# Sparse attention into a feed-forward network on one core: new costs and tables for the planner that orders the engines

## The chip, the core and the metric

The kernel runs on one core of one Trainium2 chip. The metric is the device time of one launch in microseconds (us), as a median of runs; for the kernel before it is 835.81 us (835.47 to 837.34, 3 runs). The engines are TensorE (PE; its weight loads are shown apart as PEld), VectorE (DVE), ScalarE (ACT), GpSimd (POOL), and SyncE (SP), which here only issues DMAs.

## The reference

```python
scores = scale * np.matmul(q, k.transpose(0, 1, 3, 2))    # B=8, H=8, S=576, D=64
mask_local = (rel >= 0) & (rel < 32)                      # heads 0 to 3
mask_strided = (rel >= 0) & (same residue modulo 32)      # heads 4 to 7
attn = softmax(where(mask, scores, -1e9))
x = matmul(attn, v), rearranged to 4608 tokens x 512
h = x @ w_in                                              # 512 x 2048
g = h * (1.0 / (1.0 + np.exp(-h)))
out = g @ w_out                                           # 2048 x 512
```

## The kernel before

**Arithmetic.** Every fp32 operand of the feed-forward products is split into a rounded upper part and a remainder, and a product is three matmuls (upper times upper, upper times lower, lower times upper). The upper part is a cast on ACT, the lower a subtraction on DVE: `ghi` (L757) and `glo` (L761) for the gated hidden values, `xop` pieces (L1440, L1456 on ACT, then DVE) for the first product's operands.

**Blocks.** The 4608 tokens are nine blocks of 512. For each of 16 chunks of the hidden width, blocks 0 and 1 do a first product (`hidden`, L717), a tanh (L727), a gating on DVE (L749), the two parts of the result, and a second product of 12 matmuls into four output banks (L776), which lags by one chunk. Blocks 2 to 4 take chunks two at a time by a scheme of seven half-size products, `p1` to `p7` (`multiply`, L1540, 256 columns a matmul), whose results ACT copies and DVE adds (copies L1791, L1795, L1798; tanh L1555). The words of `ORDER` and `BURST_ORDER` give the order of these seven and of the four quarters `0` to `3` of the lagging second product. A pair of chunks is called a step here; it has an index j from 0 to 7. Blocks 5 to 8 go in two pairs with 512 columns a matmul and seven products in both layers (L1540, L2093, L2222); `SUPER_ORDER` and `SUPER_BURST` give their words, and a copy on ACT (L1928) stands between some products that use the same bank.

**Weight sums.** The seven-product scheme needs sums of weight quarters. They are made during block 1, for eight f: POOL adds (L1295 to L1309), ACT casts the upper part into a slot of `xop` (L1319), DVE makes the lower (L1323), and SP stores the slot to DRAM (`keep_sum`, L1328, buffer `sums`, 512 KB each, two for each f). `xop` has six slots; four of them hold block 1's operands, so two are left, and a slot is free only when its store has landed. Later SP loads the sums into a ring (L1246). Sums for the second layer (`sum_outs`, L1379 to L1409) are made later at the steps in `OUT_SUMS`.

**Attention.** The attention of later blocks is inserted in bursts of two groups at the steps in `BURSTS` (`burst_jobs`, L1571). A burst's PE part has scores (L459, L468) and products with the values (L632) for the groups whose softmax is done. After it come DVE maxima, ACT exponentials (L526, each with a read of its sum), DVE scaling and transposes, and ACT copies of the transposed blocks (L599, to `pt`), which the *next* burst's L632 reads. ACT copies of the results are L644 and L672. ACT also moves finished output blocks from their banks to `stage` (L789), which SP stores.

**Order.** The first 130 us follow a written plan. All that follows is a list of `Job`s, each with an engine, a cost in us and the jobs it waits for; `in_order` (L1106) gives each a due time, counted back from the PE's jobs, and then plays the engines: PE's jobs in the written order, and on another engine, out of the first `LOOK` jobs, those that could start within `GRAIN` of the earliest, the one due first. Each engine executes its instructions strictly in the order so found, so a wait of the first holds up all behind it. An SP job costs `SP_ISSUE` of its queue and ends a fixed 5.0 later:

```python
firsts.append(min((f for f in found if f[0] <= start + GRAIN), key=lambda f: f[1].due))
...
free[j.engine] = t + SP_ISSUE if j.engine == "SP" else j.end
```

Of the kernel before, what the change touches and what calls it, by code (L numbers as in the profile page):

```python
# [65 lines left out]
BURSTS = {1: (1, 6, 11), 2: (1, 3, 5, 7), 3: (1, 3, 5, 7), 4: (1, 3, 5, 7), 5: (1, 3, 5)}  # L66
XORDER = ("b21", "b11", "t3", "t2", "t1", "t4", "b22")
ORDER = "p1 p7 p2 p6 0 p5 p4 1 p3 2 3"
BURST_ORDER = "0 p1 1 p7 p6 p2 p4 p5 2 3 p3"
SUPER_LAG = "p1 x x p2 p6 p7 x x p5 p4"  # L70
SUPER_FIRST = "p1 p7 p6 p2 p4 p5"
SUPER_ORDER = "p1 p7 p2 p6 p3- p4 p5"
SUPER_BURST = "p1 p3- p2 p7 B p6 p4 p5"
# [3 lines left out]
OUT_SUMS = {(2, 2): 0, (2, 4): 1, (2, 6): 2, (3, 0): 3, (3, 2): 4, (3, 6): 5, (4, 2): 6, (4, 4): 7}  # L77
# [8 lines left out]
FIRST_ORDER = "0 p7 1 p1 p2 p6 2 p5 p4 p3 3"  # L86
LOOK = 30
GRAIN = 0.04
SP_ISSUE = 0.1
# [111 lines left out]
def sparse_attention_ffn(ctx: ExitStack, tc: tile.TileContext, kqt, vt, w_in, w_out, out):  # L201
# [833 lines left out]
    class Job:  # L1035
        def __init__(self, engine, cost, act, after):
            self.engine, self.cost, self.act = engine, cost, act
            self.after, self.takes, self.late = [j for j in after if j], [], 0.0
            self.at = self.end = self.due = None
# [66 lines left out]
    def in_order():  # L1106
# [24 lines left out]
        for _ in range(PASSES):  # L1131
# [24 lines left out]
        while len(order) < len(jobs):  # L1156
# [12 lines left out]
            free[j.engine] = t + SP_ISSUE if j.engine == "SP" else j.end  # L1169
# [53 lines left out]
    def stream_on(n, p):  # L1223

        m = n + (RING if n < wide_first else WIDER)
        if m < n_sums:
            sum_loads[m] = job("SP", 5.0, lambda: load_sum(m), p, *kept_of(m))
# [56 lines left out]
    def sum_weights(f):  # L1284
# [55 lines left out]
        for i in range(2):  # L1340
# [3 lines left out]
            out.append(job("SP", 5.0, lambda i=i: keep_sum(i), l, ends=u.takes))  # L1344
# [3 lines left out]
    def sum_outs(f):  # L1348
# [51 lines left out]
        return [job("SP", 5.0, keep_sums, *l, ends=ends), kept_early.get(f) or keep_outs(f, *l)]  # L1400

    def keep_outs(f, *after):
# [8 lines left out]
        return job("SP", 5.0, act, *after)  # L1411
# [153 lines left out]
    def loads_behind(kind, i, after):  # L1565
        bufs, one = (KBUFS, load_qk) if kind == "k" else (VBUFS, load_v)
        i += bufs
        if i < len(groups) and (kind, i) not in loaded:
            loaded[kind, i] = job("SP", 5.0, lambda: one(groups[i]), after)

    def burst_jobs(c, between=lambda: None, pool="ps"):  # L1571
# [27 lines left out]
        for i, pe in zip((c, c + 1), pes):  # L1599
            value, later = groups[i], groups[i + 2] if i + 2 < len(groups) else None  # L1600
            cost = 0.33 if value.g.local else 0.62
# [8 lines left out]
            each = 0.336 if later.wide else 2 * dve(n * later.seen) / n  # L1610
            peaks = []
# [5 lines left out]
            each = 0.56 if later.wide else 0.525  # L1617
# [4 lines left out]
        for i, later, first, exps in soft:  # L1622
            n = later.g.n
            local = later.g.local
            total = job("DVE", 0.38, later.total, *exps)
# [4 lines left out]
            each = 0.36 if local else 0.43  # L1630
            turns = [job("DVE", 3 * each, lambda a=later: a.turn_in_place(), last, takes=["pt"])]
            for odd in (1, 0):
                turns.append(job("ACT", 2 * (act_of(2 * n * STRIDE)),
# [707 lines left out]
```

## Time and profile before

| | us |
|---|---|
| median of 3 runs (lowest to highest) | 835.81 (835.47 to 837.34) |
| the profiled execution, its own time | 835.76 |
| its span | 833.8 |
| PE busy | 814.8 |
| DVE busy | 632.9 |
| ACT busy | 559.7 |
| POOL busy | 70.3 |
| DMA | 182.78 MB, mean 219 GB/s |
| mean granted clock of PE | 0.992 |

The span runs from the first to the last instruction of one profiled execution; the execution's own time has some 2 us around it. A busy time says how much an engine did, not what the end waited for; that is read from the waits of PE, from the chain of waits that ended last, and from timelines of the engines where a wait stands. In a timeline, the bracket behind a row gives the idle time of that engine just before it, and what ended it.

### The profile page before, as it was taken

The numbers are of one execution on the slowest core, as the hardware profiler recorded it, in microseconds if no ns is written. First come the engines' busy times: TensorE is split into PE (matmuls) and PEld (weight loads), VectorE is DVE, ScalarE is ACT, GpSimd is POOL, SyncE is SP. The second block draws the span as 40 slices with busy tenths as digits, with TensorE's granted clock in tenths as the row PEclk, the third lists the DMA queues.
The fourth block names the chain that finished last, engine by engine and source line by source line (L and its number), as shares of the span: only waits on it lengthen the run. The fifth ranks groups of instructions, "written<-read, shape, count | busy, mean of one in ns | idle before, by whom it ended". The sixth has DMA issues, their size and how long they took to land.

```text
span 833.8 us, 19462 instructions
## 1 busy us (share of the span) xinstructions
PE 814.8 (98%) x7041; PEld 688.8 (83%) x7041; DVE 632.9 (76%) x1571; ACT 559.7 (67%) x1560; POOL 70.3 (8%) x122
## 2 busy tenths in 40 slices
PE   8899999999799999999999999999999999999998
PEld 5788878888598988888888988888888888888887
DVE  6899896675577777777778758777789984779853
ACT  7899875564677678777777768888555534555551
POOL 5300004675000000000000000000000000000000
PEclk9999999999899999999999999999999999999999
DMA  8876444378578776688876775876666788666676
GB/s 254 306 261 218 146 156 147 137 262 291 174 253 260 243 240 204 220 261 277 266 238 222 248 236 191 255 211 181 194 193 199 212 225 239 197 192 191 192 219 156
DMA packets 139007, 182.78 MB, mean 219 GB/s; under 512 B 29408, under 2 KB 82272, under 8 KB 138912
## 3 DMA queue, kind: packets, MB, share of 16 engines
q1 hardware_dynamic: 137392, 180.82, 69.8%
q8 instruction: 56, 0.92, 0.4%
q10 hardware_dynamic: 1520, 0.72, 0.3%
q14 instruction: 39, 0.32, 0.1%
HBM read 142.70 MB, written 38.80 MB: 218 GB/s over the span
## 4 chain that ended last, share of the span: by engine, by line
PE 91%; DMA 4%; ACT 2%; DVE 1%; SPq 1%; issue 1%; POOL 0%; ACTq 0%; POOLq 0%; DVEq 0%
PE ps L1540 33%; PE po L776 25%; PE po L2093 13%; PE ps L717 9%; PE ps L2093 4%; DMA sums<-xop 2%; PE ps L632 2%; PE ps L468 2%; PE po L2222 1%; DMA k<-kqt 1%; PE ps L459 1%; PE ps L885 1%; ACT pt L599 1%; PE po L632 0%; SPq L385 0%
## 5 line engine op out<-in xcount | busy, mean ns | idle before, releaser
L1540 PE MATMUL ps<-xop,w 128*128 128x256 f32 (+1 forms) x1152 | 182.6, 310 | 0.0
L1540 PEld LDWEIGHTS ps<-xop,w 128*128 128x128 f32 x1152 | 165.7, 191 | 15.5
L526 ACT ACTIVATE sm<-sm,sums 128x54 f32<-128x54 f32 (+2 forms) x320 | 109.4, 344 | 5.5 <-DVE sums L508 5.4
L717 PE MATMUL ps<-xop,w 128*128 128x512 f32 x384 | 95.2, 396 | 0.0
L776 PE MATMUL po<-w,ghi 128*128 128x512 f32 x280 | 88.5, 398 | 6.0 <-ACT ghi L757 6.0
L1540 PE MATMUL ps<-w,w 128*128 128x512 f32 x384 | 91.2, 390 | 0.0
L717 PEld LDWEIGHTS ps<-xop,w 128*128 128x128 f32 x384 | 71.8, 190 | 15.5
L1540 PEld LDWEIGHTS ps<-w,w 128*128 128x128 f32 x384 | 71.8, 188 | 14.9
L761 DVE TENSOR_TENSOR glo<-th,ghi 128x512 fp32r<-128x512 f32 x80 | 57.6, 722 | 21.2 <-ACT ghi L757 20.7
L776 PEld LDWEIGHTS po<-w,ghi 128*128 128x128 f32 x280 | 52.1, 192 | 16.1 <-ACT ghi L757 6.4
L526 ACT ACTIVATION_READ_ACCUMULATOR sm<-sm,sums 128x1 f32 x320 | 60.5, 189 | 0.0
L757 ACT CAST ghi<-th 128x512 fp32r<-128x512 f32 x78 | 48.1, 619 | 17.4 <-PE po L776 11.1
L776 PE MATMUL po<-w,glo 128*128 128x512 f32 x140 | 55.3, 395 | 0.2 <-DVE glo L761 0.2
L776 PE MATMUL po<-stage,ghi 128*128 128x512 f32 x160 | 50.5, 397 | 0.0
L2093 PE MATMUL po<-stage,w 128*128 128x512 f32 x210 | 49.2, 389 | 0.0
L2093 PEld LDWEIGHTS po<-stage,w 128*128 128x128 f32 x210 | 39.4, 188 | 8.2
L599 ACT COPY pt<-sm 32x192 f32<-32x192 f32 (+1 forms) x102 | 36.9, 362 | 2.6 <-DVE sm L591 0.4
L2093 PE MATMUL po<-v,w 128*128 128x512 f32 x162 | 38.3, 389 | 0.0
L486 POOL MEMSET sm<- 128x80 f32 (+1 forms) x18 | 2.9, 161 | 420.6 <-ACT pt L599 244.8
L776 PE MATMUL po<-v,ghi 128*128 128x512 f32 x120 | 37.9, 397 | 0.0
L749 DVE SCALAR_TENSOR_TENSOR th<-th,ps 128x512 f32<-128x512 f32 x32 | 21.6, 681 | 20.1 <-ACT th L727 20.1
L2093 PEld LDWEIGHTS po<-v,w 128*128 128x128 f32 x162 | 30.4, 188 | 6.3
(278 smaller groups left out, 1626.8 us busy)
## 6 DMA issues: line engine op xcount, KB each, us to landing
w<-sums SPq DMA_DIRECT2D x232, 256.0 KB, 2.9
w<-osums SPq DMA_DIRECT2D x104, 256.0 KB, 2.9
sums<-xop SPq DMA_DIRECT2D x16, 512.0 KB, 3.5
osums<-stage SPq DMA_DIRECT2D x16, 512.0 KB, 3.9
v<-vt SPq DMA_DIRECT2D x21, 384.0 KB, 4.0
stage<-w_out SPq DMA_DIRECT2D x14, 512.0 KB, 4.2
k<-kqt SPq DMA_DIRECT2D x14, 477.0 KB, 5.6
stage<-w_in SPq DMA_DIRECT2D x12, 512.0 KB, 4.4
```

The source lines that it names most:

```text
L459: nc.tensor.matmul(self.pss[h][rows, c * WIDE : (c + 1) * WIDE], kbd[at, 1, g.q0[t] : g.q0[t] + 2 * STRIDE], kbd[at, 0, g.k0[t] : g.k0[t] ...
L468: nc.tensor.matmul(self.pss[h][rows, c * self.seen : (c + 1) * self.seen], kbd[at, 1, g.q0[t] : g.q0[t] + g.rows], kbd[at, 0, g.k0[t] : g. ...
L526: nc.scalar.activation(out=self.s_sb[:, c, h], in_=self.s_sb[:, c, h], func=AF.Exp, bias=self.peaks[:, c, h : h + 1], scale=-1.0, accum_ou ...
L599: nc.scalar.copy(out=self.pt[to, odd], in_=of)
L632: nc.tensor.matmul(self.pso[p][h * D : (h + 1) * D, i * size : (i + 1) * size], vbd[at, 2 * i + h], moved, start=True, stop=True,)
L717: nc.tensor.matmul(ph, weight(0, wi, fc)[:, cc // 2, cc % 2 * P : (cc % 2 + 1) * P], x[xi][cc], start=(cc, n) == (0, 0), stop=(cc, n) == ( ...
L749: nc.vector.scalar_tensor_tensor(out=th[:, cols], in0=th[:, cols], scalar=1.0, in1=ph[:, cols], op0=ALU.add, op1=ALU.mult,)
L757: copy[engine](out=g[0][:, cols], in_=th[:, cols])
L761: either[engine].tensor_sub(out=g[1][:, cols], in0=th[:, cols], in1=g[0][:, cols].bitcast(F32))
L776: nc.tensor.matmul(po[tt], g[gi][:, cols], weight(1, wi, fc), start=first and n == 0, stop=last and n == 2,)
L1540: nc.tensor.matmul(bank[:, : right.shape[-1]], left(wi, kt), right[:, kt, xi], start=first and (kt, n) == (0, 0), stop=(kt, n) == (1, 2), ...
L2093: nc.tensor.matmul(bank(name, key, m), left[:, wi, m * P : (m + 1) * P], right[xi], start=first and (j, i) == (0, 0), stop=(j, i) == (FH - ...
```

## The change

The planner's model is changed, and so are the tables of words. In the model, an SP job gets a number of issues and of KB. Its queue is then taken for 0.42 us an issue, and all transfers share one server of 310 KB/us, with 2.0 us more to land. An engine counts as free 0.085 (DVE) or 0.1 us (ACT) before an operation's end; a successor on its own engine waits 0.03 and not 0.09 us. `GRAIN` grows from 0.04 to 0.25. Several costs get other values. The tables move two bursts a step later, the sums of the second layer, and products within a step. The instructions themselves are nearly the same.

```diff
-BURSTS = {1: (1, 6, 11), 2: (1, 3, 5, 7), 3: (1, 3, 5, 7), 4: (1, 3, 5, 7), 5: (1, 3, 5)}
+BURSTS = {1: (1, 7, 11), 2: (1, 3, 5, 7), 3: (2, 3, 5, 7), 4: (1, 3, 5, 7), 5: (1, 3, 5)}
-ORDER = "p1 p7 p2 p6 0 p5 p4 1 p3 2 3"
+ORDER = "p1 p7 p2 p6 0 p5 1 p4 2 p3 3"
-SUPER_ORDER = "p1 p7 p2 p6 p3- p4 p5"
-SUPER_BURST = "p1 p3- p2 p7 B p6 p4 p5"
+SUPER_ORDER = "p1 p3- p7 p6 p4 p5 p2"
+SUPER_BURST = "p1 p2 p3- p6 p7 B p4 p5"
-OUT_SUMS = {(2, 2): 0, (2, 4): 1, (2, 6): 2, (3, 0): 3, (3, 2): 4, (3, 6): 5, (4, 2): 6, (4, 4): 7}
+OUT_SUMS = {(2, 2): 0, (2, 4): 1, (2, 6): 2, (3, 2): 3, (3, 4): 4, (4, 0): 5, (4, 2): 6, (4, 4): 7}
-GRAIN = 0.04
-SP_ISSUE = 0.1
+GRAIN = 0.25
+SP_ISSUE = 0.42
+DMA_RATE = 310.0
+LANDING = 2.0
+LAP = {"DVE": 0.085, "ACT": 0.1}
...
+            self.issues, self.kb = cost if engine == "SP" else (0, 0)
+            self.cost = LANDING + self.kb / DMA_RATE if self.kb else cost
...
-            return 0.0 if a.engine in ("PE", "SP") else 0.09
+            return 0.0 if a.engine in ("PE", "SP") else 0.03
...
-                    j.due = next_due = min(j.due, next_due - j.cost)
+                    j.due = next_due = min(j.due, next_due - j.cost + LAP[engine])
...
-            free[j.engine] = t + SP_ISSUE if j.engine == "SP" else j.end
+            free[j.engine] = j.end - LAP.get(j.engine, 0.0)
+            if j.engine == "SP":
+                free["SP"] = t + SP_ISSUE * j.issues
+                free["DMA"] = max(free["DMA"], t) + j.kb / DMA_RATE
+                j.end = free["DMA"] + LANDING
...
-            out.append(job("SP", 5.0, lambda i=i: keep_sum(i), l, ends=u.takes))
+            out.append(job("SP", (1, 512), lambda i=i: keep_sum(i), l, ends=u.takes))
```

`XORDER`, `SUPER_LAG` and `FIRST_ORDER` move words in the same manner, and a dozen more jobs get other costs (an exponential 0.43 for 0.525, a scaling total 0.47 for 0.38, the two stores of an output half 1.17 for 1.25).

Three places show what it does to the order. Line numbers of the changed kernel are 3 to 9 higher.

**ACT in block 1, the first sums' cast** (L1319 before, L1328 after; the first tanh of each piece, `L727` or `L730`, is the same chunk's). Before:

```order
L526 ACTIVATE sm_2102,sums_2103<-sm_2102,sums_2103 128x96 x3
L727 ACTIVATE th_2186<-ps_2150 128x512
L526 ACTIVATE sm_2102,sums_2103<-sm_2102,sums_2103 128x96
L526 ACTIVATE sm_2168,sums_2170<-sm_2168,sums_2170 128x54
L757 CAST ghi_2201<-th_2186 128x512
L526 ACTIVATE sm_2168,sums_2170<-sm_2168,sums_2170 128x54 x6
L727 ACTIVATE th_2238<-ps_2206 128x512
L526 ACTIVATE sm_2168,sums_2170<-sm_2168,sums_2170 128x54
L1319 CAST xop_76<-stage_2147 128x4x128
L757 CAST ghi_2251<-th_2238 128x512
L1319 CAST xop_76<-stage_2147 128x4x128
```

After:

```order
L675 COPY xb_2098<-ps_2108 128x12x18
L529 ACTIVATE sm_2102,sums_2103<-sm_2102,sums_2103 128x96 x4
L1328 CAST xop_76<-stage_2141 128x4x128
L730 ACTIVATE th_2192<-ps_2151 128x512
L1328 CAST xop_76<-stage_2141 128x4x128
L529 ACTIVATE sm_2169,sums_2171<-sm_2169,sums_2171 128x54 x2
L760 CAST ghi_2207<-th_2192 128x512
L529 ACTIVATE sm_2169,sums_2171<-sm_2169,sums_2171 128x54 x6
L730 ACTIVATE th_2250<-ps_2211 128x512
```

The two casts of the first sums move from behind the second tanh to either side of the first.

**SP at the last stores of sums** (L1328 or L1337 are stores of `xop` slots, L1409 or L1418 the second layer's first sums, L1246 or L1255 loads into the ring; `sums7` is the last f). Before:

```order
L1328 DMA sums6_1964<-xop_76 128x2x512
L385 DMA v0_78<-vt 128x768
L370 DMA k0_81<-kqt 128x2x448
L1252 DMA sums7_1965<-w00_8_671 256x1x128
L1252 DMA sums7_1965<-w01_8_673 256x1x128
L385 DMA v0_78<-vt 128x512
L370 DMA k1_82<-kqt 128x2x477
L1328 DMA sums6_1964<-xop_76 128x2x512
L1409 DMA osums2_1968<-w10_0_836 128x256
...
L1409 DMA osums2_1968<-v4_1411 128x256
L1246 DMA w00_8_671<-sums0_1958 128x512 x5
L1246 DMA w00_8_671<-sums1_1959 128x512
L1328 DMA sums7_1965<-xop_76 128x2x512 x2
```

After:

```order
L1337 DMA sums6_1964<-xop_76 128x2x512 x2
L1418 DMA osums1_1967<-w10_0_836 128x256
...
L1418 DMA osums1_1967<-v4_1411 128x256
L1261 DMA sums7_1965<-w00_8_671 256x1x128
L1261 DMA sums7_1965<-w01_8_673 256x1x128
L373 DMA k0_81<-kqt 128x2x448
L388 DMA v0_78<-vt 128x768
L373 DMA k1_82<-kqt 128x2x477
L388 DMA v0_78<-vt 128x512
L1337 DMA sums7_1965<-xop_76 128x2x512 x2
L1255 DMA w00_8_671<-sums0_1958 128x512 x5
L1255 DMA w00_8_671<-sums1_1959 128x512
L1418 DMA osums2_1968<-w10_0_836 128x256
```

The last two stores of slots now stand ahead of the ring's loads and of `osums2`; before they stood behind both.

**ACT ahead of the first burst of block 4** (L599 or L602 are the copies that the burst's value products read, `th<-ps` the tanh that waits for product p3, L789 or L792 output blocks). Before:

```order
L526 ACTIVATE sm,sums<-sm,sums 128x54 x3
L1555 ACTIVATE th<-xq 128x256
L1555 ACTIVATE th<-ps 128x256
L599 COPY pt<-sm 32x192 x4
L1555 ACTIVATE th<-sm 128x512
L789 ACTIVATE stage<-po 128x4x4x32 x2
L599 COPY pt<-pt 32x192 x2
L757 CAST ghi<-th 128x512
L599 COPY pt<-sm 32x192 x2
L789 ACTIVATE stage<-po 128x4x4x32 x2
```

After:

```order
L602 COPY pt<-sm 32x192 x4
L602 COPY pt<-pt 32x192 x2
L1564 ACTIVATE th<-xq 128x256
L1564 ACTIVATE th<-sm 128x512
L602 COPY pt<-sm 32x192 x2
L1564 ACTIVATE th<-ps 128x256
L760 CAST ghi<-th 128x512
L792 ACTIVATE stage<-po 128x4x4x32 x4
```

All eight copies now stand ahead of the tanh that reads `ps` and ahead of the output blocks.

## Rows read from the trace of the kernel before

**Rows 1.** The page, section 1: busy us, share and instructions of each engine.

```profile
PE 814.8 (98%) x7041; PEld 688.8 (83%) x7041; DVE 632.9 (76%) x1571; ACT 559.7 (67%) x1560; POOL 70.3 (8%) x122
```

**Rows 2.** PE's waits over the span: waiting group, releaser: us, times, longest.

```profile
PE po L776 <- ACT ghi L757: 6.0, 1, 6.0
PE ps L632 <- ACT pt L599: 2.8, 2, 1.6
```

**Rows 3.** PE, timeline 203 to 223: start, us, operation, count, [idle <- releaser].

```profile
203.68 2.88 PE L717 MATMUL ps<-xop,w 128*128 128x512 f32 x12
...
209.12 2.88 PE L717 MATMUL ps<-xop,w 128*128 128x512 f32 x12
...
218.00 1.22 PE L776 MATMUL po<-w,ghi 128*128 128x512 f32 x2 [6.01 <-ACT ghi L757]
...
222.84 2.91 PE L717 MATMUL ps<-xop,w 128*128 128x512 f32 x12
```

**Rows 4.** Windows: length, busy of PE, PEld, DVE, ACT, POOL; clock; DMA share; GB/s.

```profile
210.00:215.00 5.00, 2.00 (x9) 1.31 (x7) 2.25 (x6) 1.18 (x6) 0.00 (x0) 1.00 0.94 308
215.00:220.00 5.00, 2.00 (x5) 1.57 (x6) 2.75 (x8) 3.22 (x12) 0.00 (x0) 0.55 0.80 289
```

**Rows 5.** ACT, timeline 209 to 218, the columns of rows 3.

```profile
209.96 0.57 ACT L727 ACTIVATE th<-ps 128x512 f32<-128x512 f32 x1
...
216.72 0.71 ACT L1440 CAST xop<-xb 128x256 fp32r<-128x256 f32 x2 [5.54 <-DMA sums<-xop]
217.34 0.61 ACT L757 CAST ghi<-th 128x512 fp32r<-128x512 f32 x1
```

**Rows 6.** SP's own queue, timeline 210 to 212.

```profile
210.05 1.04 SPq L1328 DMA_DIRECT2D sums<-xop  x2
```

**Rows 7.** POOL, then ACT, timeline 147 to 151.

```profile
150.50 0.73 POOL L1303 TENSOR_TENSOR stage<-stage 128x256 f32<-128x256 f32 x1 [10.43 <-DVE xop L1323]
...
147.06 0.61 ACT L1319 CAST xop<-stage 128x512 fp32r<-128x512 f32 x1
```

**Rows 8.** Windows, columns of rows 4: from a chunk pair's opening products to the next pair's.

```profile
242.35:265.80 23.45, 23.45 (x263) 21.10 (x262) 18.31 (x55) 18.11 (x63) 0.15 (x1) 1.00 0.76 245
312.80:340.01 27.21, 25.53 (x263) 22.62 (x262) 20.84 (x62) 21.81 (x69) 0.15 (x1) 0.94 0.73 231
410.47:435.76 25.29, 23.98 (x263) 21.37 (x262) 19.15 (x55) 20.28 (x62) 0.17 (x1) 1.00 0.79 247
```

**Rows 9.** PE, then ACT, timeline 327 to 334: first burst of block 3.

```profile
333.31 1.04 PE L632 MATMUL ps<-pt,v 64*64 64x54 f32 x30 [1.58 <-ACT pt L599]
...
327.69 0.38 ACT L1555 ACTIVATE th<-ps 128x256 f32<-128x256 f32 x1 [1.57 <-PE ps L1540]
...
332.85 0.83 ACT L599 COPY pt<-sm 32x256 f32<-32x256 f32 x2
```

**Rows 10.** PE, then ACT, timeline 425 to 431: first burst of block 4.

```profile
430.66 0.87 PE L632 MATMUL ps<-pt,v 64*64 64x54 f32 x22 [1.26 <-ACT pt L599]
...
425.36 0.38 ACT L1555 ACTIVATE th<-ps 128x256 f32<-128x256 f32 x1 [2.22 <-PE ps L1540]
...
430.26 0.72 ACT L599 COPY pt<-sm 32x192 f32<-32x192 f32 x2
```

**Rows 11.** The page, section 5: two groups of ACT (busy us, mean ns).

```profile
L526 ACT ACTIVATE sm<-sm,sums 128x54 f32<-128x54 f32 (+2 forms) x320 | 109.4, 344 | 5.5 <-DVE sums L508 5.4
...
L599 ACT COPY pt<-sm 32x192 f32<-32x192 f32 (+1 forms) x102 | 36.9, 362 | 2.6 <-DVE sm L591 0.4
```

**Rows 12.** PE, then ACT, timeline 534 to 537: a wide block.

```profile
534.54 1.66 PE L1540 MATMUL ps<-w,w 128*128 128x512 f32 x6
...
536.24 0.59 ACT L1928 COPY w<-ps 128x512 f32<-128x512 f32 x1 [0.37 <-PE ps L1540]
```

**Rows 13.** DVE, timeline 305 to 306.5.

```profile
305.19 0.69 DVE L761 TENSOR_TENSOR glo<-th,ghi 128x512 fp32r<-128x512 f32 x1 [0.22 <-ACT ghi L757]
305.80 0.68 DVE L1383 TENSOR_TENSOR stage<-stage 128x512 fp32r<-128x512 f32 x1
```

More of the change, by code (lines that the diff above doesn't have):

```diff
@@ L1036, in __init__ @@
         def __init__(self, engine, cost, act, after):
-            self.engine, self.cost, self.act = engine, cost, act
+            self.issues, self.kb = cost if engine == "SP" else (0, 0)
+            self.engine, self.act = engine, act
+            self.cost = LANDING + self.kb / DMA_RATE if self.kb else cost
             self.after, self.takes, self.late = [j for j in after if j], [], 0.0
@@ L1226, in stream_on @@
         if m < n_sums:
-            sum_loads[m] = job("SP", 5.0, lambda: load_sum(m), p, *kept_of(m))
+            sum_loads[m] = job("SP", (1, 256), lambda: load_sum(m), p, *kept_of(m))
     def kept_of(n):
@@ L1399, in sum_outs @@
         ends = [*w0.takes, *m[0].takes]
-        return [job("SP", 5.0, keep_sums, *l, ends=ends), kept_early.get(f) or keep_outs(f, *l)]
+        return [job("SP", (2, 1024), keep_sums, *l, ends=ends), kept_early.get(f) or keep_outs(f, *l)]
     def keep_outs(f, *after):
@@ L1409, in act @@
                     load(out=to[:, half], in_=of.bitcast(F32))
-        return job("SP", 5.0, act, *after)
+        return job("SP", (6, 768), act, *after)
     def operands(k, wide=False):
@@ L1568, in loads_behind @@
         if i < len(groups) and (kind, i) not in loaded:
-            loaded[kind, i] = job("SP", 5.0, lambda: one(groups[i]), after)
+            loaded[kind, i] = job("SP", (1, 460 if kind == "k" else 300), lambda: one(groups[i]), after)
     def burst_jobs(c, between=lambda: None, pool="ps"):
@@ L1600, in burst_jobs @@
             value, later = groups[i], groups[i + 2] if i + 2 < len(groups) else None
-            cost = 0.33 if value.g.local else 0.62
+            cost = 0.33 if value.g.local else 0.5
             done = [job("ACT", cost, lambda p=p, v=value: v.done_by_halves((p,)), pe)
@@ L1610, in burst_jobs @@
             each = 0.336 if later.wide else 2 * dve(n * later.seen) / n
+            if not later.g.local and c >= WIDE_FROM:
+                each = 0.62 / n
             peaks = []
@@ L1616, in burst_jobs @@
             exps = []
-            each = 0.56 if later.wide else 0.525
+            each = 0.47 if later.wide else 0.43
             for h in range(2):
@@ L1624, in burst_jobs @@
             local = later.g.local
-            total = job("DVE", 0.38, later.total, *exps)
+            total = job("DVE", 0.47, later.total, *exps)
             size = 0.75 if local else (0.61 if n == 4 else 0.5)
@@ L1629, in burst_jobs @@
             first.takes[1].last.append(last)
-            each = 0.36 if local else 0.43
-            turns = [job("DVE", 3 * each, lambda a=later: a.turn_in_place(), last, takes=["pt"])]
+            turns = [job("DVE", 0.9 if local else 1.1, lambda a=later: a.turn_in_place(), last, takes=["pt"])]
             for odd in (1, 0):
-                turns.append(job("ACT", 2 * (act_of(2 * n * STRIDE)),
+                turns.append(job("ACT", 0.82 if local else 0.93,
                                  lambda a=later, odd=odd: a.turn_across(odd), turns[-1]))
@@ L1674, in save @@
                         store(k, state["po", k], some)
-                    place = job("ACT", 1.25, save, made[-1], takes=["stage"])
-                    end = job("SP", 4.0, lambda: None, place, ends=place.takes)
+                    place = job("ACT", 1.17, save, made[-1], takes=["stage"])
+                    end = job("SP", (1, 256), lambda: None, place, ends=place.takes)
                     stored[k].append(place)
@@ L1686, in sparse_attention_ffn @@
             if i < len(groups):
-                loaded[kind, i] = job("SP", 5.0, lambda i=i, kind=kind: (load_qk if kind == "k" else load_v)(groups[i]))
+                loaded[kind, i] = job("SP", (1, 400), lambda i=i, kind=kind: (load_qk if kind == "k" else load_v)(groups[i]))
     quarters = ((0, 1), (2, 3))
@@ L1745, in sparse_attention_ffn @@
             for n in range(RING):
-                sum_loads[n] = job("SP", 5.0, lambda n=n: load_sum(n), *kept_of(n), *free)
+                sum_loads[n] = job("SP", (1, 256), lambda n=n: load_sum(n), *kept_of(n), *free)
     own_first.last += [last_hidden, *free]
@@ L2131, in act @@
                     )
-            out["place"].last.append(job("SP", 5.0, act, *after))
+            out["place"].last.append(job("SP", (4, 256), act, *after))
         def keep(self, which, name, made):
```

12 lines of the change are left out of this document (6 added, 6 removed).

## The prediction

> **What bounds the kernel.** I read the page first: PE is busy 814.8 us of a span of 833.8, and no other engine comes near it [rows 1]. So PE's work is the floor, and what a new order can give is idle time of PE and PE time at a lower clock. The waits of PE come second. Two groups matter: 6.0 us once, for `ghi` ahead of the second product, and 2.8 us in two pieces, for the copies `pt` ahead of a burst's value products [rows 2]. After 500 us that view shows no wait at all. The third view is the granted clock in windows of 5 and 10 us. From 40 us on it is 1.00 (2.4 GHz), but for the 25 us around the first wait and some 10 us behind the second. So each of these waits costs more than its idle time, because PE afterwards runs for a while at the lower level (1.2 GHz). I therefore price a wait by the whole distance between two equal places of the program, less the same distance where nothing was late.
>
> **Term A, the wait in block 1.** In an ordinary chunk the hidden products start 5.44 us apart (203.68 to 209.12). The next such start comes at 222.84, 13.72 later [rows 3]. The excess is 13.72 - 5.44 = **8.28 us**: 6.01 idle, and the rest in matmuls at half clock (clock 0.55 in 215 to 220) [rows 3, 4]. The cause is in ACT's order. Two casts of the next block's operand (L1440) stand ahead of the cast to `ghi`, and they wait 5.54 us for a slot of `xop` that a store of weight sums still reads; the `ghi` cast runs at 217.34, 0.66 before PE goes on [rows 5]. That store was issued at 210.05 [rows 6], and its slot came free at 216.72 [rows 5], with the DMA engines 0.94 busy at 308 GB/s [rows 4]. PE wanted `ghi` at 218.00 - 6.01 = 211.99. Take off the two L1440 pairs' 0.62 us of lead and about 1.5 us for the casts and DVE's part: the slot has to be free by about 209.8, that is 6.9 us sooner.
>
> Two moves work on this. The first casts of sums run at 147.06, and POOL stands idle 10.43 us until 150.50 for them [rows 7]. In the new order they stand on either side of the first tanh of that stretch, and no longer behind the second; one chunk is 5.44 [rows 3], so POOL's chain of eight starts about 5.4 to 6.4 sooner. And SP now issues the last two stores ahead of six ring loads of 256 KB and six quarter loads of `osums2`; the ring alone is 1.57 MB, which takes 5.1 us at 308 GB/s [rows 4]. Together that is 10.5 to 11.5 us if nothing eats it. The later casts wait for the same two slots, so I allow 2 us of loss: the slot is free between 206 and 208, 2 to 4 us ahead of the need. Either move alone (5.4 or 5.1) would leave a wait of 1 to 2 us. I take all 8.28.
>
> **Term B, the first burst of block 3.** A cycle of two steps with one burst takes 23.45 us from the opening products of one step pair to the next; the cycle with this burst takes 27.21 [rows 8]. The excess is **3.76 us**: a wait of 1.58 at 333.31, some 0.8 us more idle in smaller pieces, and half clock after it. What PE waits for is the last copy L599, which runs at 332.85 because ACT stood 1.57 us on the tanh that needs product `p3`, with ready copies behind it, and then moved output blocks [rows 9]. The change puts this burst one step later, so that ACT has a further step for the copies, and I count the excess as gone.
>
> **Term C, the first burst of block 4.** The same mechanism: 25.29 against 23.45 [rows 8], **1.84 us**, a wait of 1.26 with the last copy at 430.26, behind 2.22 us on the same tanh [rows 10]. In the new order all eight copies precede that tanh and the output blocks. They need some 8 x 0.36 = 2.9 us [rows 11], and the 2.22 us in which ACT stood are theirs now. Gone too.
>
> **What else moves, and what covers it.** The matmuls, casts, copies and DMAs are nearly the same ones, so no engine's busy sum changes by more than a few operations. SP's new spacing is only in the model: the real issues take what they took. If the model holds a transfer back, PE feels it only where a load is late; no wait for a load stands in the list of PE's waits past the start. Moved second-layer sums (POOL is idle, DVE 18.31 of 23.45 [rows 8]) cost nothing while their ring loads come steps later.
>
> In block 3 two bursts now follow each other in successive steps, and the second's value products need the first's copies. The exponentials and reads of two groups are 12 x 0.344 = 4.1 us, the copies 2.9 [rows 11], result copies and the step's own casts and tanhs about as much again. One step has 23.45/2 = 11.7 us [rows 8]. By ACT's new order I count the last copy about 1.2 us ahead of the need. If it fails, the nearest rows are terms B and C: 1.84 to 3.76. I take 0, since the order puts these copies ahead of their tanh, and keep both ends.
>
> In blocks 5 to 8 the new words leave one product between `p7` and `p4`, and between `p6` and `p5`, for the copy that frees the value they share. No row of before has this wait. A gain is excluded, since PE waits nowhere there. For the price: a matmul of 512 columns takes 5.44/24 = 0.227 us [rows 3], a product of six 1.36, so PE comes back 2.72 us after the first began. In the trace the product began at 534.54 and the copy ended at 536.24 + 0.59 = 536.83 [rows 12], 2.29 after: 0.4 us to spare. With one other ACT operation of 0.6 in front the wait is 0.2, with none 0. There are 22 such places (two in each of 11 steps). The bounds are 0 and 22 x 0.2 = 4.4; I take 0, as in the new ACT order these copies stand first at nearly all of them.
>
> **Sum.** 835.76 (the profiled execution's own time, 0.05 under the median) - 8.28 - 3.76 - 1.84 = 821.88. I forecast **822.0 us**.
>
> **A rule against this.** The plan now lets DVE begin an operation 0.085 us ahead of the end of the one before. In the trace L761 starts at 305.19 and lasts 0.69, and L1383 starts at 305.80, 0.08 ahead of its end [rows 13]. So the sum goes by the plan's lap. The Trainium skill, "VectorE: DVE Perf Modes", section "The DRAIN you can't avoid", says that the next DVE operation does not start until the pipe of the one before has emptied. By that rule the plan would promise DVE results too soon; the row disagrees, and what it would cost is the last rival.
>
> **Rivals.**
> - *One late hand-off is left or is new* (the second of the close bursts, some copies of the wide blocks, or a rest of A of 1 to 2 us). For it: the margins of 0.4 and 1.2 us above. Against it: the copies' places in the order. Price 1.84 to 3.76: 823.7 to 825.6.
> - *Term A stays*, because the stores still land late: the DMA engines are 0.94 busy there [rows 4], and a store sent sooner shares them with other transfers. Then only B and C are gone: 835.76 - 5.60 = 830.2.
> - *The order does nothing*: the waits come from transfers or clock, whatever the order. Against it: each wait's releaser is an ACT operation that was ready and stood behind another [rows 5, 9, 10]. 835.8.
> - *Slower: the wide blocks' hand-offs.* Two ACT operations of 0.6 ahead of each copy make a wait of 1.2 - 0.4 = 0.8 at 22 places, 17.6 us, and lower clock on top. It turns the sign from 13.88/22 = 0.63 us a place. 821.9 + 17.6 = 839.5. For it: ACT still has 12 exponentials there behind each burst. Against it: they end within some two steps of a burst, and most places have none in front.
> - *Slower: DVE has no lap.* Then 55 operations a cycle [rows 8] are 0.085 later each, 4.7 us by the cycle's end, and DVE has 23.0 of 23.45 full. Each of the twelve bursts of blocks 2 to 4 would be late as in C: 821.9 + 12 x 1.84 = 844.0. Rows 13 speak against it.
>
> **Chances.** The forecast has 0.62, one late hand-off 0.20, A staying 0.06, no effect 0.04, the wide hand-offs 0.06, no lap 0.02. What a measurement can tell from no change here is about 0.2%, 1.7 us. So faster 0.88, same 0.04, slower 0.08. The range holds the first two cases, 0.82: from 820.3 (1.6 below the sum, for the half clock behind smaller waits that I did not price) to 826.8 (the dearer late hand-off and 1.2 us of small waits).
>
> **What would show it.** PE's list of waits should hold neither `ghi` 6.0 nor `pt` 2.8, and the clock should be 1.00 in every window from 40 us on. In block 1 all hidden starts should be 5.44 apart but for bursts, the last store of a slot issued by about 201, and POOL resuming near 144. The cycles of blocks 3 and 4 should all last 23.4 to 23.6. I am wrong if a wait for `xop` still ends on a store after 210, if the value products of burst (3, 3) wait for `pt`, or if L1540 or L2093 wait for the copy L1928 in the wide blocks. Wrong by another path would be a wait of PE for a load.

## The result and the profile after

The changed kernel takes 821.79 us (median; 819.82 to 824.26, 4 runs) against 835.64 (835.02 to 837.34, 4 runs): a ratio of 0.9833, with a 95% interval of 0.9802 to 0.9864. The forecast was 822.0, with 820.3 to 826.8. The number is right; some of the steps that led to it are not, and the experiments below show which.

The waits of PE over the whole span of the changed kernel (waiting group, releaser: us, times, longest):

```profile
PE po L620 <- issue: 3.2, 2, 2.4
```

This group and five smaller ones all lie in the first 31 us. From 131 us to the end the view shows no wait of PE at all; the two groups of [rows 2] are gone. The granted clock is 1.00 in every window of 10 us from 40 to 820. The page's first section, to hold against [rows 1]:

```profile
PE 811.3 (99%) x7041; PEld 686.5 (84%) x7041; DVE 638.5 (78%) x1571; ACT 557.5 (68%) x1560; POOL 74.3 (9%) x122
```

**A measure without the start.** The profiled execution of the changed kernel took 824.26 us, the longest of its four, and its span is 822.0. Its start was a long one. The written plan of the first 130 us is the same in both kernels, and yet the last hidden product ahead of block 1's first burst begins at these times (PE's timeline of the kernel before, then of the changed one):

```profile
129.48 2.88 PE L717 MATMUL ps<-xop,w 128*128 128x512 f32 x12
```

```profile
131.69 2.88 PE L720 MATMUL ps<-xop,w 128*128 128x512 f32 x12
```

So the new execution lost 2.21 us where nothing was changed. In 14 profiles of 14 kernels this point lies between 126.8 and 131.7 us. I call the time from it to the end of the span **the rest**: 833.8 - 129.48 = 704.3 before, 822.0 - 131.69 = 690.3 after. The difference is 14.01 us, against a sum of 13.88 from three terms. All further comparisons of profiles use the rest. Each rest comes from one profiled execution, so the medians are kept beside it.

**Term A.** The hidden products behind the last stores, in the changed kernel (PE's timeline; [rows 3] answer to them):

```profile
210.81 2.88 PE L720 MATMUL ps<-xop,w 128*128 128x512 f32 x12
...
216.58 2.88 PE L720 MATMUL ps<-xop,w 128*128 128x512 f32 x12
```

The distance is 216.58 - 210.81 = 5.77, where 5.44 is the plain one: 0.33 is left of 8.28. ACT's timeline shows how near it was ([rows 5] before):

```profile
208.35 0.60 ACT L730 ACTIVATE th<-ps 128x512 f32<-128x512 f32 x1 [1.80 <-PE ps L720]
212.17 0.71 ACT L1449 CAST xop<-xb 128x256 fp32r<-128x256 f32 x2 [3.22 <-DMA sums<-xop]
212.79 0.62 ACT L760 CAST ghi<-th 128x512 fp32r<-128x512 f32 x1
```

The first two operand casts (L1449) still stand ahead of `ghi` and still wait for a store, 3.22 us. SP's queue ([rows 6] before):

```profile
203.45 0.90 SPq L1337 DMA_DIRECT2D sums<-xop  x2
204.45 6.69 SPq L1255 DMA_DIRECT2D w<-sums  x6
```

The two stores went out at 203.45, which is 71.8 behind the fixed point; before it was 210.05 - 129.48 = 80.6. They are 8.8 us sooner. But the slot came free only 212.17 - 203.45 = 8.7 us after the issue, where it took 6.7 before [rows 5, 6]; six ring loads were issued right behind. The slot is 6.8 us sooner, and 6.9 were needed.

**Terms B and C.** The windows of the changed kernel that answer to [rows 8] (length, busy of PE, PEld, DVE, ACT, POOL; clock; DMA share; GB/s). The first is two cycles, with both close bursts of block 3; the second holds the first burst of block 4:

```profile
306.52:353.43 46.91, 46.91 (x522) 42.32 (x522) 37.24 (x110) 37.92 (x127) 0.32 (x2) 1.00 0.77 241
400.49:423.95 23.46, 23.46 (x262) 21.08 (x262) 19.21 (x54) 19.98 (x64) 0.17 (x1) 1.00 0.64 202
```

46.91 is twice 23.46; before, the same two cycles took 363.46 - 312.80 = 50.66 (27.21 of it [rows 8]). The second is 23.46 against 25.29. ACT ahead of the burst in block 4, which begins at 418.04:

```profile
412.33 1.45 ACT L602 COPY pt<-sm 32x192 f32<-32x192 f32 x4 [1.50 <-DVE sm L594]
...
415.84 0.72 ACT L602 COPY pt<-sm 32x192 f32<-32x192 f32 x2
416.76 0.38 ACT L1564 ACTIVATE th<-ps 128x256 f32<-128x256 f32 x1 [0.19 <-PE ps L1549]
```

The last copies are done at 416.56, ahead of the tanh on `p3`, 1.5 us before the burst; before, the last one began at 430.26 with PE waiting [rows 10].

By these windows the three terms gave 7.95, 3.75 and 1.83, together 13.53 of the 14.01; where the other 0.48 lies was not looked for.

### The profile page after: what moved, and what is told of

The parts are those of the page before. It is cut to its first block, busy times and chain, and to the rows that moved or that the text cites. A ratio compares the mean times of both kernels' runs of the same rounds, so it can differ in the third digit from the quotient of the medians.

```text
span 822.0 us, 19441 instructions
## 1 busy us (share of the span) xinstructions
PE 811.3 (99%) x7041; PEld 686.5 (84%) x7041; DVE 638.5 (78%) x1571; ACT 557.5 (68%) x1560; POOL 74.3 (9%) x122
## 4 chain that ended last, share of the span: by engine, by line
PE 97%; POOL 1%; issue 1%; DVE 0%; POOLq 0%
PE ps L1549 33%; PE po L779 27%; PE po L2103 13%; PE ps L720 11%; PE ps L2103 4%; PE ps L635 3%; PE po L2232 1%; PE ps L471 1%; PE ps L462 1%; PE po L620 0%; PE po L635 0%; POOL v L399 0%; POOL mask_strided L240 0%; POOL mask__94 L240 0%; PE po L554 0%
## 5 line engine op out<-in xcount | busy, mean ns | idle before, releaser
L1549 PE MATMUL ps<-xop,w 128*128 128x256 f32 (+1 forms) x1152 | 185.5, 310 | 0.0
L1549 PE MATMUL ps<-w,w 128*128 128x512 f32 x384 | 93.7, 389 | 0.0
L764 DVE TENSOR_TENSOR glo<-th,ghi 128x512 fp32r<-128x512 f32 x80 | 59.3, 743 | 12.4 <-ACT ghi L760 10.5
L779 PEld LDWEIGHTS po<-w,ghi 128*128 128x128 f32 x280 | 50.4, 189 | 8.9 <-ACT ghi L760 0.2
L602 ACT COPY pt<-sm 32x192 f32<-32x192 f32 (+1 forms) x102 | 36.9, 362 | 5.5 <-DVE sm L594 3.5
L1564 ACT ACTIVATE th<-sm 128x512 f32<-128x512 f32 x30 | 18.9, 632 | 29.7 <-DVE sm L1812 24.4
L1942 DVE TENSOR_TENSOR w<-ps,w 128x512 f32<-128x512 f32 x33 | 22.7, 688 | 20.3 <-PE ps L1549 16.3
```

The lines of the kernel that those rows point to most:

```text
L602: nc.scalar.copy(out=self.pt[to, odd], in_=of)
L764: either[engine].tensor_sub(out=g[1][:, cols], in0=th[:, cols], in1=g[0][:, cols].bitcast(F32))
L779: nc.tensor.matmul(po[tt], g[gi][:, cols], weight(1, wi, fc), start=first and n == 0, stop=last and n == 2,)
L1549: nc.tensor.matmul(bank[:, : right.shape[-1]], left(wi, kt), right[:, kt, xi], start=first and (kt, n) == (0, 0), stop=(kt, n) == (1, 2), ...
L1564: nc.scalar.activation(out=th[:, cols], in_=h, func=AF.Tanh, scale=0.5)
L1942: nc.vector.tensor_add(out=to, in0=of(), in1=to)
```

## The experiments

Twelve kernels, each profiled once and timed in three rounds together with the kernel before. The first column of numbers is the rest, by which they are compared. Each ratio below is against the runs of the kernel before that belong to it; their medians were 834.52, 835.34 and 835.02 in the three sets of experiments, within 831.43 to 838.89. The gain over the kernel before by the rest and by those medians agrees within 2.2 us, and a difference of two kernels smaller than that is read from windows and not from either.

| kernel | the rest, us | minus the kernel before | median us (runs) |
|---|---|---|---|
| before | 704.3 | | 835.64 (4) |
| the change | 690.3 | -14.0 | 821.79 (4) |
| new model, old tables | 690.8 | -13.6 | 822.05 (4) |
| old model, new tables | 699.9 | -4.4 | 831.11 (10) |
| change, block 3's burst back | 690.4 | -13.9 | 822.48 (4) |
| change, block 1's burst back | 691.6 | -12.7 | 821.79 (4) |
| new model without server | 698.1 | -6.3 | 830.05 (4) |
| new model without laps | 694.8 | -9.5 | 823.70 (4) |
| before with the server alone | 697.2 | -7.1 | 826.40 (4) |
| before with laps and grain | 700.8 | -3.5 | 831.74 (4) |
| before, casts behind `ghi` | 698.1 | -6.2 | 829.34 (5) |
| before, ring loads last | 697.7 | -6.6 | 829.41 (7) |
| change, casts behind `ghi` | 690.1 | -14.3 | 821.46 (4) |
| before, grain and casts | 703.0 | -1.3 | 833.05 (10) |

### Model or tables

**New model, old tables.** Only the constants that are tables go back.

```diff
-BURSTS = {1: (1, 7, 11), 2: (1, 3, 5, 7), 3: (2, 3, 5, 7), 4: (1, 3, 5, 7), 5: (1, 3, 5)}
+BURSTS = {1: (1, 6, 11), 2: (1, 3, 5, 7), 3: (1, 3, 5, 7), 4: (1, 3, 5, 7), 5: (1, 3, 5)}
...
-SUPER_ORDER = "p1 p3- p7 p6 p4 p5 p2"
+SUPER_ORDER = "p1 p7 p2 p6 p3- p4 p5"
```

> The new model with all the old tables. In its order the L599 copies of the first bursts of blocks 3 and 4 stand ahead of the tanh on product p3 and ahead of the output blocks, and the last two stores of sums ahead of the ring loads, but the first cast of sums stays behind the second tanh. Theory (the order found by the model decides): terms B and C are gone (both cycles 23.4 to 23.6), and of A's 8.28 a wait of about 1.8 is left (6.9 needed less 5.1 for the stores' place), priced 2 to 3: 824 to 825. Rival (the tables of words and burst steps decide): B and C stay in full, 830 or more.

Measured: 822.05 us, ratio 0.9843 (0.9807 to 0.9878), rest 690.8. B and C are gone as the theory said, but for 0.4 of B (cycles of 23.81 and 23.44), but so is A, where I expected 2 to 3 us to be left. PE's waits from 60 us on, then ACT, SP and POOL of this kernel:

```profile
PE po L779 <- DVE glo L764: 0.3, 1, 0.3
```

```profile
205.84 0.62 ACT L760 CAST ghi<-th 128x512 fp32r<-128x512 f32 x1 [0.22 <-DVE th L752]
207.86 0.71 ACT L1449 CAST xop<-xb 128x256 fp32r<-128x256 f32 x2 [1.40 <-DMA sums<-xop]
```

```profile
200.76 1.05 SPq L1337 DMA_DIRECT2D sums<-xop  x2
```

```profile
148.41 0.73 POOL L1312 TENSOR_TENSOR stage<-stage 128x256 f32<-128x256 f32 x1 [7.55 <-DVE xop L1332]
```

POOL resumes 148.41 - 127.05 = 21.4 us behind the fixed point, as late as before (150.50 - 129.48 = 21.0). And yet the last stores go out 73.7 behind it, 6.9 sooner than before, so they do not need the first cast's new place. But this run does not show that the sooner stores are enough: the `ghi` that was held up before now runs at 205.84, ahead of the operand casts, and their wait of 1.40 for a store holds up nothing that PE needs next. Sooner stores and another order on ACT came together here; the runs below part them.

**Old model, new tables.** The reverse: the kernel before with all the new tables and nothing of the model.

```diff
-BURSTS = {1: (1, 6, 11), 2: (1, 3, 5, 7), 3: (1, 3, 5, 7), 4: (1, 3, 5, 7), 5: (1, 3, 5)}
+BURSTS = {1: (1, 7, 11), 2: (1, 3, 5, 7), 3: (2, 3, 5, 7), 4: (1, 3, 5, 7), 5: (1, 3, 5)}
...
-SUPER_ORDER = "p1 p7 p2 p6 p3- p4 p5"
+SUPER_ORDER = "p1 p3- p7 p6 p4 p5 p2"
```

> All new tables with the old model. In its order the first cast of sums stands early, beside the first tanh, but the last two stores stand behind the ring loads; before burst (4, 1) the last two copies stand behind the tanh on p3 again. Theory: B gone with the burst's place, C stays (1.84), and of A about 1.5 us of wait is left (6.9 less 5.4), priced 2: 825 to 826. Rival (tables alone carry the gain): 822.

Measured: 831.11, ratio 0.9948 (0.9929 to 0.9967), dearer than the 825 to 826 I had expected. B is gone but for some 0.8 us (the two cycles take 47.74), and of C 1.1 is left (24.61). For B the later burst did what the prediction said of it: the last copy ended at 333.05, and the burst began at 337.08. A is not gone: PE's longest waits, then ACT.

```profile
PE po L776 <- ACT ghi L757: 4.8, 2, 3.7
```

```profile
206.10 0.62 ACT L1319 CAST xop<-stage 128x512 fp32r<-128x512 f32 x1 [4.07 <-DMA sums<-xop]
...
214.71 0.71 ACT L1440 CAST xop<-xb 128x256 fp32r<-128x256 f32 x2 [4.79 <-DMA sums<-xop]
```

Here POOL resumed at 140.19, 13.4 behind this run's fixed point (126.80), 7.6 sooner than before, and it did not help: the casts of sums and the operand casts wait for stores (4.07 and 4.79), and the last stores go out 81.6 behind the point, no sooner than before. This is the second run that denies the first cast its part in A.

### The bursts' steps

**Block 3's burst back to step 1**, in the changed kernel.

```diff
-BURSTS = {1: (1, 7, 11), 2: (1, 3, 5, 7), 3: (2, 3, 5, 7), 4: (1, 3, 5, 7), 5: (1, 3, 5)}
+BURSTS = {1: (1, 7, 11), 2: (1, 3, 5, 7), 3: (1, 3, 5, 7), 4: (1, 3, 5, 7), 5: (1, 3, 5)}
```

> The changed kernel with block 3's first burst put back from step 2 to step 1. In its order all copies of that burst stand ahead of the tanh on p3 and of the output blocks, as before burst (4, 1). Theory (the copies' place in ACT's order decides): B stays gone, cycle 23.4 to 23.6, 822. Rival (the step of the burst decides, as the prediction's term B says): the cycle takes up to 27.2 and the time is 824 to 825.6.

Measured: 822.48, ratio 0.9849 (0.9817 to 0.9881). The window with that burst at its old step, and ACT ahead of its value products, which began at 323.64:

```profile
305.55:329.02 23.47, 23.47 (x262) 21.10 (x262) 19.40 (x58) 20.96 (x71) 0.15 (x1) 1.00 0.67 201
```

```profile
321.61 0.83 ACT L602 COPY pt<-sm 32x256 f32<-32x256 f32 x2
322.46 0.38 ACT L1564 ACTIVATE th<-ps 128x256 f32<-128x256 f32 x1
```

23.47, and no wait for `pt`: the last copies stand ahead of the tanh on `p3`. With the new model the burst's step is not needed to remove B. With the old model the new tables, the step among them, removed most of it too (0.8 left of 3.76). So B has two ways out, and in the change they overlap.

**Block 1's burst back to chunk 6**, in the changed kernel.

```diff
-BURSTS = {1: (1, 7, 11), 2: (1, 3, 5, 7), 3: (2, 3, 5, 7), 4: (1, 3, 5, 7), 5: (1, 3, 5)}
+BURSTS = {1: (1, 6, 11), 2: (1, 3, 5, 7), 3: (2, 3, 5, 7), 4: (1, 3, 5, 7), 5: (1, 3, 5)}
```

> The changed kernel with block 1's second burst put back from chunk 7 to chunk 6. In its order the first cast of sums goes back behind the second tanh, and the last two stores stand among and behind the ring loads, as in the kernel before. Theory (the place of the cast and of the stores decides A): A comes back for the most part, a wait for ghi of 3 to 6 us, 826 to 830. Rival (the server alone makes the stores land in time): 822 to 823.

Measured: 821.79, ratio 0.9837 (0.9800 to 0.9875), and one wait of 0.8 for `glo` from 60 us on. The theory fails: the last two stores went out at 202.47 and 204.44, among ring loads, 74.2 and 76.2 behind the point, and still sooner than before. A place among the ring loads does not by itself bring A back.

### The parts of the model

**New model without the server**, old tables: SP's jobs cost again what they did.

```diff
-                free["SP"] = t + SP_ISSUE * j.issues
-                free["DMA"] = max(free["DMA"], t) + j.kb / DMA_RATE
-                j.end = free["DMA"] + LANDING
+                free["SP"] = t + 0.1
+                j.end = t + 5.0
```

> All old tables and the new model, but SP jobs cost what they did before (0.1 us of queue, end 5.0 us after the issue, no server). The order of ACT ahead of the bursts of blocks 3 and 4 is that of the run with the new model; five ring loads and a sixth stand ahead of the last two stores of sums again. The measure is the time from the last hidden product ahead of block 1's first burst to the end of the span: 704.3 before, 690.3 for the change, 690.8 for the new model with the old tables. Theory (the server in the model settles A, the rest of the model B and C): A comes back, 693 to 699. Rival (the server does nothing, the durations and laps do all): 690 to 691.

Measured: 830.05, ratio 0.9939 (0.9923 to 0.9956), rest 698.1, as the theory said. PE's waits, SP and ACT:

```profile
PE po L779 <- ACT ghi L760: 5.0, 1, 5.0
```

```profile
204.59 3.26 SPq L1336 DMA_DIRECT2D sums<-xop  x2
```

```profile
212.55 0.71 ACT L1448 CAST xop<-xb 128x256 fp32r<-128x256 f32 x2 [6.91 <-DMA sums<-xop]
...
215.74 0.62 ACT L760 CAST ghi<-th 128x512 fp32r<-128x512 f32 x1 [0.44 <-DVE th L752]
```

No other wait is left: B and C need no server. Against the run with it, A costs 698.1 - 690.8 = 7.3. The time of issue alone does not explain that. The two stores went out at 204.59 and 207.48, 75.2 and 78.1 behind the point: sooner than before (80.6), and the first of them only 1.0 later than in the run with block 1's burst back, which had no wait for `ghi`. But the first slot came free 8.0 us after its issue, 83.1 behind the point (81.2 in that run), and here all four operand casts and a tanh stand ahead of that `ghi`, where two casts stood before.

**New model without laps**, old tables.

```diff
-LAP = {"DVE": 0.085, "ACT": 0.1}
+LAP = {"DVE": 0.0, "ACT": 0.0}
```

> All old tables and the new model with its server, but with no lap: an engine counts as taken to an operation's end. The copies stay ahead of the tanh on p3 at both bursts, but the model, which sees ACT and DVE busier, puts the last stores of sums behind ring loads and quarter loads. Theory: B and C stay gone and A comes back in part or in full: 692 to 699 by the measure of the run without the server. Rival (laps matter only for B and C): 694 to 696 with waits for pt and none for ghi.

Measured: 823.70, ratio 0.9861 (0.9847 to 0.9876), rest 694.8, in the range of both, and by neither's waits:

```profile
PE ps L1549 <- DVE sums L511: 1.0, 2, 0.5
PE ps L635 <- DVE th L1559: 0.9, 1, 0.9
```

There is no wait for `ghi` and none for `pt`, but, with two smaller ones for `xop`, 2.8 us in places that had none. By the rests the laps are worth 694.8 - 690.8 = 4.0 us, of which 2.6 lie in the two cycles of B and C (25.33 and 24.48, against 23.81 and 23.44). By the medians it is 823.70 - 822.05 = 1.65, so the size of the whole is not settled. And A is gone but for 0.6 (hidden products 6.05 apart) with the last stores later than ever (210.80 and 214.75, 83.8 and 87.7 behind the point 127.01):

```profile
210.80 0.37 SPq L1337 DMA_DIRECT2D sums<-xop  x1
...
214.75 0.40 SPq L1337 DMA_DIRECT2D sums<-xop  x1
```

```profile
207.77 0.62 ACT L1328 CAST xop<-stage 128x512 fp32r<-128x512 f32 x1 [3.18 <-DMA sums<-xop]
...
215.11 1.33 ACT L1449 CAST xop<-xb 128x256 fp32r<-128x256 f32 x4
```

The operand casts run at 215.11, without a wait of their own and behind the `ghi` they held up before (208.30). They start 0.36 us after the last store went out, so they cannot have waited for its slot. So there is a second way out of A, which the prediction did not have.

**Before with the server alone**, old tables, durations and grain, no laps.

```diff
+LAP = {"DVE": 0.0, "ACT": 0.0}
...
-            free[j.engine] = t + SP_ISSUE if j.engine == "SP" else j.end
+            free[j.engine] = j.end - LAP.get(j.engine, 0.0)
+            if j.engine == "SP":
+                free["SP"] = t + SP_ISSUE * j.issues
+                free["DMA"] = max(free["DMA"], t) + j.kb / DMA_RATE
+                j.end = free["DMA"] + LANDING
```

> The kernel before with the server for transfers and the issues of SP alone: old tables, old durations, old grain, no laps. ACT's order ahead of the first bursts of blocks 3 and 4 is that of before. Theory: B and C stay (5.6 together), and A stays at least in part, as one of the last stores stands behind ring and quarter loads: 697 to 704 by the same measure. Rival (the server alone settles A): 696.

Measured: 826.40, ratio 0.9899 (0.9876 to 0.9921), rest 697.2 (the median is 8.9 under that of the kernel before, the rest only 7.1). The rival was nearer: no wait for `ghi` is left, and those for `pt` are as before.

```profile
PE ps L635 <- ACT pt L602: 2.8, 2, 1.6
```

```profile
207.94 0.38 SPq L1337 DMA_DIRECT2D sums<-xop  x1
...
214.25 0.37 SPq L1337 DMA_DIRECT2D sums<-xop  x1
```

```profile
206.56 0.62 ACT L760 CAST ghi<-th 128x512 fp32r<-128x512 f32 x1 [0.25 <-DVE th L752]
...
213.55 1.33 ACT L1449 CAST xop<-xb 128x256 fp32r<-128x256 f32 x4 [0.43 <-DMA sums<-xop]
```

Again the stores are no sooner (79.9 and 86.2 behind 128.07). The server tells the planner when the slot will be free, and it puts the `ghi` that was held up before (206.56), and the next one (211.65), ahead of the casts that have to wait (213.55).

**Before with laps, the larger grain and the shorter own wait**, no server, old durations.

```diff
-GRAIN = 0.04
+GRAIN = 0.25
+LAP = {"DVE": 0.085, "ACT": 0.1}
...
-            return 0.0 if a.engine in ("PE", "SP") else 0.09
+            return 0.0 if a.engine in ("PE", "SP") else 0.03
```

> The kernel before with laps, the larger grain and the shorter wait on the own engine, without the server and without most of the new durations; old tables. In ACT's order all copies of the first burst of block 3 stand ahead of the tanh on p3, and six of eight at block 4. Theory: B gone, C gone or small, A stays as the ring loads stand ahead of the last two stores: 695 to 700 by the same measure. Rival (measured durations are what brings the copies forward): B and C stay, 699 to 704.

Measured: 831.74, ratio 0.9956 (0.9941 to 0.9971), rest 700.8, 0.8 above the theory's range. A stays, and B and C are down to 0.7 and 0.4 (cycles of 24.19 and 23.82) without the server and without the measured durations:

```profile
PE po L779 <- ACT ghi L760: 6.7, 1, 6.7
```

### What A hangs on

**Before, casts behind `ghi`.** A hint to the planner, nothing else.

```diff
-            u = job("ACT", act_of(2 * size) + 0.2 * n, upper, *after[half], takes=ring_of(name))
+            first = [state["last_ghi"]] if k == 2 else []
+            u = job("ACT", act_of(2 * size) + 0.2 * n, upper, *after[half], *first, takes=ring_of(name))
...
     lags = [lag, rest_lag]
+    state["last_ghi"] = lag[1]
```

> The kernel before; the planner alone is told that block 2's two raw operand casts (L1440) come after the ghi cast of block 1's last chunk but one. PE's, DVE's and SP's order ahead of it and the stores' place stay as before; in ACT's order the casts stand behind the ghi they held up. Measure as before: 704.3 for the kernel before. Theory now (A is a cast that stood ahead of ghi on ACT; the stores may land as late as they did): no wait for ghi, 8.3 less, 696.0; B and C stay. Rival (the prediction's: the stores have to land 6.9 us sooner, else block 2's operands are late and PE waits there instead): a wait of PE for xop at block 2's start, 699 to 704.

Measured: 829.34, ratio 0.9935 (0.9909 to 0.9960), rest 698.1: 6.2 of the 8.3. The stores went out as late as before (209.32, 81.4 behind 127.97):

```profile
PE po L776 <- ACT ghi L757: 0.8, 1, 0.8
```

```profile
207.03 0.62 ACT L1319 CAST xop<-stage 128x512 fp32r<-128x512 f32 x1 [5.14 <-DMA sums<-xop]
...
210.78 0.62 ACT L757 CAST ghi<-th 128x512 fp32r<-128x512 f32 x1
```

The 6.0 are down to 0.8, and that is a cast of sums, which now waits 5.14 ahead of `ghi`. The waits for `pt` stay (2.9). The operand casts run from 216.33 on, and PE waits 0.34 for block 2's first operand. Most of A was thus the order on ACT: with the stores as late as before, moving the casts was enough.

**Before, ring loads last.** The other way alone.

```diff
-            free = [*raws, *(kept_parts[f, 6][0] for f in range(FH)), h]
+            free = [*raws, *(kept_parts[f, 6][0] for f in range(FH)), h, *kept[-1][1]]
```

> The kernel before; the planner alone is told that the ring loads come after the last stores of sums. The first cast of sums also stands earlier in the order it finds, and the casts that wait for a slot still stand ahead of ghi. Theory now and the prediction's alike (sooner stores are a second way): the last stores go out some 7 us sooner and the wait for ghi falls from 6.0 to below 1.5, 696 to 698. Rival (the stores' place does nothing; transfers share the same engines whatever their order): 703 to 705.

Measured: 829.41, ratio 0.9944 (0.9923 to 0.9965), rest 697.7. The stores went out at 202.35, 72.7 behind 129.66, and the wait is 1.5:

```profile
PE po L776 <- ACT ghi L757: 1.5, 1, 1.5
```

This edit moved other stores too, the planner being one whole, so it shows that sooner stores do (the operand casts still stand ahead of `ghi` here), not that the ring loads alone were in the way.

**The change, casts behind `ghi`.** Both ways together; the same hint in the changed kernel.

> The changed kernel with the same hint: casts behind ghi. Theory: the rest of A, 0.33 us at the hidden product behind the last store, goes too, 690.0 by the measure (690.3 for the change) and within 0.2% of it in time. Rival (the casts are late now and block 2 starts late): 691 or more.

Measured: 821.46, ratio 0.9843 (0.9815 to 0.9871), rest 690.1. The hidden products stand 5.44 apart to the last:

```profile
208.45 2.88 PE L720 MATMUL ps<-xop,w 128*128 128x512 f32 x12
...
213.89 2.88 PE L720 MATMUL ps<-xop,w 128*128 128x512 f32 x12
```

The 0.33 are gone. In time this version cannot be told from the change.

**Before, grain and casts.** Two small edits to have it all.

```diff
-GRAIN = 0.04
+GRAIN = 0.25
```

and the hint above.

> The kernel before with two small edits alone: the grain of 0.25 for 0.04, and the hint that puts the casts behind ghi. In its order all copies stand ahead of the tanh on p3 at block 3, six of eight at block 4, in both with two output blocks ahead of the last pair. Theory (the three waits are places in ACT's order and nothing else is worth having): A and B gone, C 0 to 1.8, 690 to 692.5. Rival (the measured durations and the server are needed for it): 694 or more.

Measured: 833.05, ratio 0.9974 (0.9953 to 0.9995), rest 703.0. My theory fails clearly. PE's waits:

```profile
PE ps L1541 <- ACT xop L1457: 2.2, 1, 2.2
PE po L776 <- ACT ghi L757: 1.5, 2, 1.1
```

The long waits are gone, and new or remaining ones come to 7.3 us in seven groups, 2.2 us for a later operand cast and 1.1 for `pt` among them. That a wait is only a place in an order does not mean that it can be had alone.

## Why the prediction was right, and where it was not

**The bound and the method.** Right. Pricing each wait by the distance of equal places gave 13.88; the rest fell by 14.01. The listed waits alone, 8.8 us, would have been too little: 5.0 of the 13.88 is time that the list does not show, 2.3 in A, 2.2 in B and 0.6 in C. In A and B the granted clock was below 1.00 there [rows 4, 8]. One reading of B is wrong: there is no "0.8 us more idle" behind its wait of 1.58, for PE's idle time in that cycle is 27.21 - 25.53 = 1.68 in all [rows 8]; the rest is slower matmuls.

**Term A, size right, working wrong in two places.** The step "so POOL's chain of eight starts about 5.4 to 6.4 sooner" came true (POOL resumed at 147.40, 5.3 sooner behind the fixed point) and had no effect: new model with old tables resumes POOL as late as before, sends the last stores 6.9 sooner and has no A; old model with new tables resumes it 7.6 sooner and keeps A. And the step "the slot is free between 206 and 208, 2 to 4 us ahead of the need" was off: set back by the 2.21 us of the start, it came free at 209.96, 0.2 after the need of 209.8. I had the issue right (201.24 on that scale, "by about 201"), and had let the store take as long as before or less; it took 8.7 us where the old one took 6.7. Of the sooner issue, 8.8 us, the longer store thus took back 2.0. By its letter the prediction's own sign of being wrong, a wait for `xop` that ends on a store after 210, came true (212.17; 209.96 with the start taken off). The forecast of 0 for the rest of A was thus luck by a narrow margin; 0.33 was left. What the text missed altogether is the second way: with the server the planner also knows that the slot will be late, and may put `ghi` first. Without the server, stores that went out 5.4 and 2.5 sooner left a wait of 5.0. Three runs removed A or most of it with stores about as late as before or later.

**Term B, size right, cause not needed.** "The change puts this burst one step later, so that ACT has a further step for the copies" is one way to the gain (old model, new tables: 0.8 left), but the change does not depend on it: with the burst at its old step the cycle takes 23.47. As in term C, the new model puts the copies ahead of the tanh. The word "same mechanism" of term C should have made me ask why C goes without a move.

**Term C.** Right in size: 1.83 us, and the copies stand ahead of the tanh. No run moved the copies of B or C alone, so that their place is what removes the two waits is read from the timelines. With the new model they stand ahead of that tanh and of the output blocks, and PE does not wait for `pt`; in the last run those of block 3 stood ahead of the tanh but behind two output blocks, and 0.6 of wait was left.

**What was costed at nothing.** Right. The close bursts of block 3 take two plain cycles, PE has no wait in the wide blocks, and no load became late. The new tables together are worth 690.8 - 690.3 = 0.5 us on top of the new model, which one profile of each cannot tell from nothing.

**The rule that was weighed.** Without laps the plan was 4.0 us worse by the rest and 1.65 by the medians. Had each DVE operation waited for the end of the one before, a plan without laps would have been the truer one; the run agrees with [rows 13], but it took ACT's lap away too and so does not show DVE's share. The section of the Trainium skill that the prediction names ("VectorE: DVE Perf Modes", "The DRAIN you can't avoid") also says that a next operation that is not held starts earlier, which I had left out: by that sentence the early start in [rows 13] is no exception, and the rival was weaker than I wrote it.

**Open.** Why the store took 8.7 us was not tried by itself; that the ring loads issued a microsecond behind it share its engines is argued from the order of issues. Without the server, how much of the 5.0 us is the late slot and how much the longer row of casts ahead of `ghi` was not taken apart. Nor was which of laps, grain and own wait brings the copies forward, nor why the two small edits of the last run bring new waits.

## What to carry to other kernels

In a planned order, price a stall by the distance between equal places, then ask which operation stood ready behind a waiting one: that place is the stall, and a planner that knows when transfers land moves it without being told. Several parts of a model then give the same stall back by different ways, so undo each part before crediting one of them. Compare profiles from a point behind the start, where the start alone varies by more than some of the effects, and hold what one profile says against the medians.

## What was not expected of the hardware

The start, with the same written plan in all kernels, ended between 126.8 and 131.7 us behind the first instruction, a spread of 4.9 us; in the changed kernel's profile two waits of PE of together 3.2 us had no releaser that the profile shows. The last two stores (2 x 512 KB) kept the first slot for 6.7 us in the kernel before, 8.7 in the changed one and 8.0 without the server.
